# Quarter loads of expert weights, later reads of turned columns, and a rearranged attention prologue in a fused attention and expert kernel

## The chip, the core and the metric

The kernel runs on one core of a Trainium2 chip. The core has five engines with an instruction stream each: TensorE (PE: matmuls and transposes into PSUM), VectorE (DVE), ScalarE (ACT), GpSimd (POOL) and SyncE (SP, which only issues transfers here). They share the on-chip memory SBUF and meet through semaphores; every engine works through its own stream in order. Sixteen DMA engines move data. Transfers are issued by SyncE, ScalarE and GpSimd, each with a queue of its own. The metric is device time of one execution in microseconds, the median of several runs.

## What is computed

A polynomial sketch attention feeds a layer of experts chosen by a hash of the token number. Cut to what matters:

```python
# q, k, v: (4 batches, 4 heads, 1088 rows, 32); S1, S2: (8, 32)
phi(x) = outer(S1 x, S2 x)                  # 64 features of a row and head
kv, z  = sum_s phi(k)_s v_s^T, sum_s phi(k)_s
attn   = (phi(q) kv) / (phi(q) z + 1e-6)
x      = attn as rows: (4352, 128)          # the four heads side by side
e      = token_ids * 2654435761 % 8         # the expert of each row
out    = relu(x @ w1[e]) @ w2[e]            # w1: (8, 128, 1024), w2: (8, 1024, 128), float32
```

## The kernel before

**Attention.** One batch after the other. The 1024 main rows of a batch are eight tiles of 128, and 64 tail rows of each batch are kept in tiles of their own. For k and q, 128 x 128 blocks are turned on TensorE (`turned_all`, evicted by ScalarE), multiplied by the sketch matrix (`s_products`), and the outer product is made on VectorE in two products of 1024 columns (`features`, L512: `f` for q, `kp` for k). `values` (L532) copies v into a tile with a column of ones, on GpSimd. `kv_products` (L541) sums k's features times v, `q_turned` (L558, L565) turns q's features, `x_products` (L577) multiplies, `denominators` and `x_main`/`x_tail` (L603, L611) divide and store the rows to DRAM (`x_rows`). The loop `for b in range(B - 1)` (L757) works on the products of batch b and the features of batch b + 1; before it stand batch 0's first stages, k and q of batch 1 turned, and the tails' products and features (L732 to L746).

**Routing.** Beside the attention, VectorE and GpSimd work out where each row goes. `route_slots` gives a place, `route_rows` and `route_tiles` (L401) make 0/1 matrices for row and tile of that place, `tiles` (L411, L416, both on GpSimd) carries the token numbers in two parts, and `route_list` (L421) multiplies them on TensorE to a list `get` of tokens in the order of their experts, and `put`, where results go. Experts are taken in the order of how many rows are left beyond 256, from a table `order` that is worked out at run time; so a weight load first reads a register from `order` on the engine that issues it (`load_expert`).

**Experts.** There are 16 groups of rows: groups 0 to 7 have 256 rows each, one for each expert and only of batches 0 and 1; groups 8 to 15 hold the rest, 320 down to 271 rows. A group has eight steps c: `layer1(g, c)` (L837) makes 128 of the 1024 hidden columns and a ReLU evicts them, on ScalarE for even c and on VectorE for odd c (L623, L625); `layer2(g - 1, c)` (L845) adds the step's share of the group before. Four PSUM banks take turns in layer 1, two in layer 2.

Around these steps stand, at places written by hand as `at(group, step, function)`:

- `fetch_tile(k, j)`: gathers 128 rows by index on GpSimd (L617), its index copied on VectorE (`paced`, L677) to hold the gather back.
- Incoming rows are turned into columns: chunks 0 and 1 on TensorE (`bring`, L688), the others by `turn_in(k)`: VectorE splits them into halves of 16 bits (L696), SyncE issues one DMA transpose (L697), and `join_in(k)` puts them together again (L702, VectorE).
- Outgoing columns: ScalarE evicts in halves (L885), `turn_out` issues two DMA transposes on SyncE (L898), `join_out` joins them on VectorE (L906), `scatter_next` writes 128 rows by index from GpSimd (L848).
- `load_expert(r, ...)`: the two layers of the expert of rank r, 512 KB each. Ranks 0 to 2 go from SyncE; ranks 3 to 7 from ScalarE at step 2 of groups 1 to 5.
- `x_main`, `x_tail` of batches 2 and 3 on GpSimd, with their stores, in groups 1 and 2.

The order of each engine's instructions is that of the code (a manual schedule). VectorE waits in place when a joined tile has not landed, with the ReLUs behind it.

Of the kernel before, what the change touches and what calls it, by code (L numbers as in the profile page):

```python
# [9 lines left out]
F32 = mybir.dt.float32  # L10
BF16 = mybir.dt.bfloat16
I32 = mybir.dt.int32
# [18 lines left out]
def kernel(  # L31
# [13 lines left out]
    P = 128  # L45
# [102 lines left out]

    at_rank = {}
# [8 lines left out]
    q_tail = load_tail(q, "q_tail")  # L158
    k_t.append(load_main(k, 1, "k"))
    q_t.append(load_main(q, 1, "q"))  # L160
    v_tail = load_tail(v, "v_tail")
# [203 lines left out]
    def route_slots(digits):  # L365

        V_ = nc.vector
        late, slot, gap, over = (const.tile([P, C], F32, name=n) for n in ("late", "slot", "gap", "over"))
# [9 lines left out]
        V_.scalar_tensor_tensor(slot[:], slot[:], float((E - 1) * GE - (E - 2) * GAP), gap[:], op0=OP.add, op1=OP.add)  # L378
        V_.tensor_tensor(slot[:], slot[:], late[:], op=OP.mult)
# [28 lines left out]

    def route_tiles():
        hot(in_tile[:], number[:, 0:SE], st[:, 0])  # L410
        nc.gpsimd.tensor_tensor(tiles[:, :, 1].rearrange("p c (n x) -> p c n x", x=2),  # L411
                                in_tile[:].rearrange("p c (n x) -> p c n x", x=2),
                                twice[:].unsqueeze(2).to_broadcast([P, C, SE // 2, 2]), op=OP.mult)

    def route_tiles_p():
        nc.gpsimd.tensor_scalar(tiles[:, :, 0], in_tile[:], p1[:], None, op0=OP.mult)  # L416
# [113 lines left out]
    def values(b, copy=nc.gpsimd.tensor_copy):  # L530

        copy(vas[b % 2][:, :, :, 0:D], v_t[b][:].rearrange("p h t d -> p t h d"))  # L532
# [140 lines left out]
    def paced(idx):  # L673


        t = rows_in.tile([P, 1], I32, tag="idx", name="idx", bufs=4)
        nc.vector.tensor_copy(t[:], idx)  # L677
        return t[:]
# [43 lines left out]
    values(0)  # L722
# [6 lines left out]
    first_copied(aq, abq, range(GQ))  # L729
    kv = kv_products(0, kp, range(T))  # L730
    features(f, aq, abq, range(GQ))
    tail_ps = bank([P, 2, TT, P], "tail_ps")  # L732
    tail_turned(k_tail, tail_ps, 0)
    tail_turned(q_tail, tail_ps, 1)
    tailT = work.tile([P, 2, TT, P], F32, tag="fT", name="tailT", bufs=1)
    nc.scalar.copy(tailT[:], tail_ps[:])
# [3 lines left out]
    kT = turned_all(k_t[1], "kT")  # L740
    abt = tail_products(tailT)
    tail_features(abt)
    qT = turned_all(q_t[1], "qT")
    for u, va_tail in enumerate(va_tails):
        rows = tail_rows(u * TT)
        nc.gpsimd.tensor_copy(va_tail[rows, :, :, 0:D], v_tail[rows])  # L746
# [10 lines left out]
    for b in range(B - 1):  # L757
# [6 lines left out]
        if b == 0:  # L764
            k_t.append(load_main(k, 2, "k", A.memzero))
            q_t.append(load_main(q, 2, "q"))
            tail_f_turned()
            route_slots(digits)
        elif not last:
            qT = turned_all(q_t[b + 1], "qT")  # L770
# [3 lines left out]
        kv = kv_products(b, kp, range(T if b == 0 else 0, T + 1), kv if b == 0 else None)  # L774
        m = kv_diagonal(b, kv)
# [6 lines left out]
        values(b + 1)  # L782
        if b == 1:
            v_t.append(load_main(v, 3, "v", A.memzero))
            load_expert(0, (1,))
            route_rows(0)
            route_tiles()
            route_tiles_p()
            route_rows(1)
        features(f, aq, abq, range(GQ))  # L790
        x_products(b, fT, m)
# [5 lines left out]
        if b == 1:  # L797
            load_expert(0, (2,), A.memzero)
            load_expert(1, (1,))
        if b > 0:  # L800
            features(kp, ak, abk, range(GQ))
            denominators(b)
        else:
            denominators(b)
            features(kp, ak, abk, range(GQ))
        if not last:
            for g in range(GQ):
                x_main(b, g, nc.gpsimd)
            x_tail(b, nc.gpsimd)
        if last:  # L810
            for j in range(tiles_of(0)[1]):
                fetch_tile(0, j, True)

# [5 lines left out]
    load_expert(1, (2,), A.memzero)  # L819
    last_m = kv_diagonal(e, kv)  # L820
    for j in range(2):
        fetch_tile(1, j)

# [78 lines left out]
    def join_out():  # L902
        i, n, tts = turned_out.pop()
# [62 lines left out]
    for c in range(2):  # L966
        at(0, 3 + 2 * c, fetch_tile, 2, c)
    at(0, 4, load_expert, 2, (1, 2), lambda x: nc.vector.memset(x, 0.0))
    at(0, 6, bring, 1, o_bank)
    for g in range(1, E - 2):  # L970
        at(g, 2, load_expert, g + 2, (1, 2), None, nc.scalar, ENG.Activation)


    ahead = [(k, j) for k in range(3, 11) for j in range(tiles_of(k)[1])]
    for g, n in enumerate((0, 4, 4, 2, 2, 2, 2, 2)):
        for c in range(n):
            at(g, 1 + c, fetch_tile, *ahead.pop(0))
    assert not ahead

    for b, g in ((B - 2, 1), (e, 2)):  # L980
        for i in range(GQ):
            at(g, 5, x_main, b, i, nc.gpsimd, nc.gpsimd)
        at(g, 6, x_tail, b, nc.gpsimd, nc.gpsimd)
# [166 lines left out]
```

## Time and profile before

| | us |
|---|---|
| three runs | 191.65, 193.06, 193.37 |
| median | 193.06 |
| profiled execution, whole | 195.57 |
| its span, first to last instruction | 193.8 |
| attention until the first layer-1 product | 0 to 51.2 |
| experts | 51.2 to 193.8 |
| mean granted TensorE clock | 0.98 |

Durations below come from the profiled execution, 2.5 us longer than the median. Its page gives busy shares, the span in 40 slices (4.85 us each, a digit being tenths), and groups of instructions. In rows in order of time the columns are: start, length, engine, line and operation with its tiles and shapes, the number of instructions merged into the row, and in brackets how long the engine stood idle before it and what ended that. Lengths of merged rows run from the first start to the last end. What one execution spent in full-flow steps can be seen from 110 to 180 us, where TensorE is busy all the time:

```profile
65.40:98.70 33.30, 25.99 (x109) 21.46 (x108) 13.30 (x38) 7.78 (x22) 23.04 (x26) 0.95 0.73 187
110.00:180.00 70.00, 70.00 (x290) 54.44 (x289) 32.60 (x117) 19.27 (x52) 35.24 (x35) 1.00 0.30 69
```

Each row is a stretch (from, to, length), the busy time of TensorE, of its weight loads, of VectorE, ScalarE and GpSimd with their instruction counts, the granted clock, the share of the DMA engines, and GB/s.

### The profile page before, as it was taken

How to read it: one execution, taken by the hardware profiler on the slowest of the kernel's cores; microseconds unless marked ns; L12 is line 12 of the kernel's file. 1: busy time of each engine (PE TensorE's matmuls, PEld its weight loads, DVE VectorE, ACT ScalarE, POOL GpSimd, SP SyncE). 2: the span in 40 equal slices, each digit the busy share in tenths (PEclk: the TensorE clock that was granted, in tenths of full speed). 3: DMA queues.
4: the chain of work that ended last, by engine and by line, in shares of the span. 5: the costliest groups of instructions: out<-in, count | busy, mean ns of one | idle time of the engine just before them, and what ended most of it. 6: DMA issues, size and time to landing. Idle time of an engine off the chain costs nothing. (4 is left out here: it accounts for less than half of the span.)

```text
span 193.8 us, 4260 instructions
## 1 busy us (share of the span) xinstructions
PE 173.5 (90%) x1567; PEld 144.6 (75%) x1567; DVE 102.1 (53%) x291; ACT 63.2 (33%) x171; POOL 106.6 (55%) x145
## 2 busy tenths in 40 slices
PE   7788999799999569796959999999999999999990
PEld 3687999799887458575848888777777777778990
DVE  5786999989442283334233465263344654525330
ACT  3626674706352202222311332322313313231320
POOL 7251298974421877876526665644666444054752
PEclk9999999999999979999997999999999999999999
DMA  4994667961248927993889333414224052140111
GB/s 133 250 250 109 215 213 254 311 230 30 68 129 230 244 83 213 229 286 87 206 230 213 68 86 81 98 39 97 67 54 97 27 122 60 20 99 26 41 33 32
DMA packets 38678, 25.96 MB, mean 134 GB/s; under 512 B 21252, under 2 KB 35717, under 8 KB 38656
## 3 DMA queue, kind: packets, MB, share of 16 engines
q1 hardware_dynamic: 29952, 14.75, 29.1%
q0 software_dynamic: 2624, 5.64, 10.2%
q10 hardware_dynamic: 6080, 5.28, 10.0%
q8 instruction: 13, 0.21, 0.5%
q14 instruction: 9, 0.07, 0.1%
HBM read 17.41 MB, written 4.52 MB: 113 GB/s over the span
## 5 line engine op out<-in xcount | busy, mean ns | idle before, releaser
L845 PE MATMUL op<-hT,w 128*128 128x256 f32 (+8 forms) x256 | 78.2, 396 | 0.0
L625 DVE TENSOR_SCALAR hT<-hp 128x256 f32<-128x256 f32 (+9 forms) x68 | 29.0, 426 | 54.0 <-PE hp L837 44.3
L848 POOL DMA_INDIRECT out_dram<-os,put x35 | 35.3, 1008 | 40.2 <-DVE os L906 22.8
L845 PEld LDWEIGHTS op<-hT,w 128*128 128x128 f32 x256 | 48.6, 194 | 11.1
L623 ACT ACTIVATE hT<-hp 128x256 f32<-128x256 f32 (+9 forms) x68 | 26.6, 390 | 78.1 <-PE hp L837 76.6
L837 PE MATMUL hp<-xT,w 128*128 128x256 f32 x128 | 39.9, 401 | 9.8 <-DVE xT L702 6.0
L617 POOL DMA_INDIRECT xg<-x_rows,idx x33 | 33.7, 1020 | 23.1 <-DVE idx L677 11.2
L837 PE MATMUL hp<-xT_late,w 128*128 128x320 f32 (+8 forms) x144 | 41.7, 385 | 0.0
L837 PEld LDWEIGHTS hp<-xT,w 128*128 128x128 f32 x128 | 24.7, 199 | 15.7 <-DVE xT L702 6.8
L837 PEld LDWEIGHTS hp<-xT_late,w 128*128 128x128 f32 x144 | 25.3, 190 | 6.7
L906 DVE COPY os<-turned 128x256 uint16<-128x256 uint16 (+1 forms) x26 | 8.6, 358 | 9.1 <-DMA turned<-half 8.8
L696 DVE COPY xh<-xg 128x256 uint16<-128x256 uint16 (+1 forms) x28 | 9.0, 362 | 3.8 <-DMA xg<-x_rows,idx 3.8
L512 DVE TENSOR_TENSOR f<-first_of_ab,ab_ps 128x1024 f32<-128x1024 f32 x8 | 9.4, 1212 | 0.9 <-ACT first_of_ab L505 0.9
L512 DVE TENSOR_TENSOR kp<-first_of_ab,ab_ps 128x1024 f32<-128x1024 f32 x8 | 9.3, 1204 | 0.6 <-ACT first_of_ab L505 0.6
L541 PE MATMUL kv<-va,kp 128*64 128x33 f32 x256 | 8.4, 224 | 0.7 <-POOL va L532 0.7
L541 PEld LDWEIGHTS kv<-va,kp 128*64 128x64 f32 x256 | 7.9, 138 | 1.4 <-POOL va L532 0.8
L603 POOL TENSOR_TENSOR xs<-xe,den 128x512 f32<-128x512 f32 x8 | 8.3, 1055 | 0.7 <-DVE den L597 0.6
L702 DVE COPY xT<-xh_turned 128x256 uint16<-128x256 uint16 x12 | 4.9, 458 | 6.8 <-DMA xh_turned<-xh 6.6
L577 PE MATMUL x_ps<-m,fT 128*64 128x66 f32 x256 | 8.3, 222 | 0.0
L577 PEld LDWEIGHTS x_ps<-m,fT 128*64 128x64 f32 x256 | 7.9, 137 | 0.3 <-issue 0.3
L558 PE MATMUL fT_ps<-ident,f 128*128 128x128 f32 x64 | 7.9, 276 | 0.0
L885 ACT COPY half<-op 128x256 uint16<-128x256 uint16 x16 | 5.2, 375 | 7.3 <-PE op L845 7.3
(184 smaller groups left out, 171.3 us busy)
## 6 DMA issues: line engine op xcount, KB each, us to landing
w<-in_moe_w_dram ACTq DMA_DIRECT2D x10, 512.0 KB, 4.6
w<-in_moe_w_dram SPq DMA_DIRECT2D x6, 512.0 KB, 5.2
q<-in_q_dram SPq DMA_DIRECT2D x4, 512.0 KB
v<-in_v_dram SPq DMA_DIRECT2D x4, 512.0 KB, 6.9
k<-in_k_dram SPq DMA_DIRECT2D x3, 512.0 KB
x_rows<-xs SPq DMA_DIRECT2D x4, 256.0 KB, 4.0
x_rows<-xs POOLq DMA_DIRECT2D x4, 256.0 KB, 3.9
out_dram<-os,put POOLq DMA_INDIRECT x35, 2.8
```

The lines of the kernel that those rows point to most:

```text
L512: nc.vector.tensor_tensor(dst[:].rearrange("p t h i j -> p (t h) i j")[:, r], a[:, r].unsqueeze(3).to_broadcast(shape), rows_of_ab(ab)[:, ...
L541: nc.tensor.matmul(kv[h * R * R:(h + 1) * R * R, pr], f[:, 2 * pr + h].rearrange("p i j -> p (i j)"), v_[:, 2 * pr + h], start=(t == 0 and ...
L577: nc.tensor.matmul(p[r, t, 2 * pr:2 * pr + 2].rearrange("p h d -> p (h d)"), fT[:, lo + t, pr, r], m[:, pr].rearrange("p h d -> p (h d)"), ...
L603: eng.tensor_tensor(rows_of[b][:, r], xes[b % 2][:, r, 0:D], dens[b][:, r].unsqueeze(2).to_broadcast([P, Q * H, D]), op=OP.mult)
L617: nc.gpsimd.indirect_dma_start(out=dst, out_offset=None, in_=x_dram[0:rows], in_offset=bass.IndirectOffsetOnAxis(ap=idx, axis=0), bounds_c ...
L623: nc.scalar.activation(dst, src, AF.Relu if relu else AF.Copy)
L625: return nc.vector.tensor_scalar(dst, src, 0.0, None, op0=OP.max).ins
L696: nc.vector.tensor_copy(xh[:, x * w:(x + 1) * w], _half(xg3[k][:].rearrange("p a b -> p (a b)")[:, 0:w], x))
L837: nc.tensor.matmul(hp[:, 0:hi - lo], w1[:, g % E, c * P:(c + 1) * P], x_columns(first_of(g) + lo, first_of(g) + hi), start=True, stop=True)
L845: nc.tensor.matmul(ops[g][:, 0:hi - lo], w2[:, g % E, c], hTs[g][:, c, lo:hi], start=(c == 0), stop=(c == FC - 1))
L848: st_ = nc.gpsimd.indirect_dma_start(out=out[:], out_offset=bass.IndirectOffsetOnAxis(ap=idx, axis=0), in_=src, in_offset=None, bounds_che ...
L906: nc.vector.tensor_copy(_half(os[:].rearrange("p a b -> p (a b)"), x)[:, 0:n * DM], tts[x][:, 0:n].rearrange("p a b -> p (a b)"))
```

## The change

- **Weights.** `load_half` loads half a layer of an expert (256 KB, a quarter of the expert) from SyncE behind a VectorE memset of the destination's first column, which places it in time. In groups 1 to 6 the second layer of rank g + 1 comes at steps 0 and 3, the first layer of rank g + 2 at steps 4 and 7. Whole loads remain for ranks 0 and 1 and the first layer of rank 2, some at other places. Nothing is loaded from ScalarE any more.
- **Turned columns.** `turn_in(k)` moves to step 3 of group k - 2 (step 6 for k = 3 and k from 9), `join_in(k)` to step 4 of group k - 1. `join_out` moves to step 0 of the following group for g below 8, with the scatters after it; two turned tiles can be open, so the oldest is taken (`pop(0)`). Chunk 2 is turned on TensorE at (1, 5). Gathers move accordingly; their index tiles are eight instead of four.
- **Rows of batch 2** are divided on VectorE after the last `kv_diagonal`; those of batch 3 on GpSimd in group 0. Both are stored from SyncE.
- **Token numbers.** Of the two products that make `tiles`, one goes to VectorE, the other to ScalarE; the 0/1 matrix they need is made earlier, before the `kv_products` of batch 1.
- **Prologue.** Half of the first `values` goes to ScalarE, q's tail is loaded after the second q, and the tails are turned and made into features inside the first turn of the loop. `route_slots` is cut in two, `route_parts` coming first.

```diff
+    def load_half(r, layer, x):
+        load_expert(r, ())
+        e = at_rank[r]
+        if layer == 1:
+            r1 = slice(x * F // 2, (x + 1) * F // 2)
+            nc.vector.memset(w1[:, r, r1.start:r1.start + 1], 0.0)
+            nc.sync.dma_start(w1[:, r, r1], moe_w1[bass.ds(e, 1)].rearrange("o p f -> p (o f)")[:, r1])
+        else:
+            r2 = slice(x * FC // 2, (x + 1) * FC // 2)
+            nc.vector.memset(w2[:, r, r2.start, 0:1], 0.0)
+            nc.sync.dma_start(w2[:, r, r2], moe_w2[bass.ds(e, 1)].rearrange("o (c p) d -> p (o c) d", p=P)[:, r2])
...
     k_tail = load_tail(k, "k_tail")
-    q_tail = load_tail(q, "q_tail")
     k_t.append(load_main(k, 1, "k"))
     q_t.append(load_main(q, 1, "q"))
+    q_tail = load_tail(q, "q_tail")
...
+    def route_in_tile():
+        hot(in_tile[:], number[:, 0:SE], st[:, 0])
     def route_tiles():
-        hot(in_tile[:], number[:, 0:SE], st[:, 0])
-        nc.gpsimd.tensor_tensor(tiles[:, :, 1].rearrange("p c (n x) -> p c n x", x=2),
+        nc.vector.tensor_tensor(tiles[:, :, 1].rearrange("p c (n x) -> p c n x", x=2),
...
     def route_tiles_p():
-        nc.gpsimd.tensor_scalar(tiles[:, :, 0], in_tile[:], p1[:], None, op0=OP.mult)
+        nc.scalar.activation(tiles[:, :, 0], in_tile[:], AF.Copy, scale=p1[:])
...
-        t = rows_in.tile([P, 1], I32, tag="idx", name="idx", bufs=4)
+        t = rows_in.tile([P, 1], I32, tag="idx", name="idx", bufs=8)
...
-    values(0)
+    values(0, slice(0, T // 2))
...
     first_copied(aq, abq, range(GQ))
+    values(0, slice(T // 2, T), nc.scalar.copy)
...
         if b == 0:
...
-            tail_f_turned()
-            route_slots(digits)
+            tail_ps = bank([P, 2, TT, P], "tail_ps")
+            tail_turned(k_tail, tail_ps, 0)
+            tail_turned(q_tail, tail_ps, 1)
+            tailT = work.tile([P, 2, TT, P], F32, tag="tailT", name="tailT", bufs=1)
+            nc.scalar.copy(tailT[:], tail_ps[:])
+            qT = turned_all(q_t[1], "qT")
...
+            values(1)
+            route_parts(digits)
+            tail_features(tail_products(tailT))
...
+        if b == 1:
+            route_in_tile()
+            route_tiles_p()
...
         if b == 1:
             load_expert(0, (2,), A.memzero)
-            load_expert(1, (1,))
...
+        if b == 1:
+            load_expert(1, (1,))
         if last:
             for j in range(tiles_of(0)[1]):
                 fetch_tile(0, j, True)
+            load_expert(1, (2,), A.memzero)
...
-    load_expert(1, (2,), A.memzero)
     last_m = kv_diagonal(e, kv)
+    load_expert(2, (1,), A.memzero)
     for j in range(2):
         fetch_tile(1, j)
+    for g in range(GQ):
+        x_main(e - 1, g, V)
+    x_tail(e - 1, V)
...
-        i, n, tts = turned_out.pop()
+        i, n, tts = turned_out.pop(0)
...
     for c in range(2):
-        at(0, 3 + 2 * c, fetch_tile, 2, c)
-    at(0, 4, load_expert, 2, (1, 2), lambda x: nc.vector.memset(x, 0.0))
+        at(0, c, fetch_tile, 2, c)
+    for c in range(2):
+        at(0, 3 + c, fetch_tile, 3, c)
     at(0, 6, bring, 1, o_bank)
-    for g in range(1, E - 2):
-        at(g, 2, load_expert, g + 2, (1, 2), None, nc.scalar, ENG.Activation)
+    at(1, 5, bring, 2)
+    for g in range(1, E - 1):
+        for x in range(2):
+            at(g, 3 * x, load_half, g + 1, 2, x)
+            if g + 2 < E:
+                at(g, 4 + 3 * x, load_half, g + 2, 1, x)
...
-    ahead = [(k, j) for k in range(3, 11) for j in range(tiles_of(k)[1])]
-    for g, n in enumerate((0, 4, 4, 2, 2, 2, 2, 2)):
+    ahead = [(k, j) for k in range(4, 11) for j in range(tiles_of(k)[1])]
+    for g, n in enumerate((0, 2, 4, 4, 2, 2, 2)):
...
-    for b, g in ((B - 2, 1), (e, 2)):
-        for i in range(GQ):
-            at(g, 5, x_main, b, i, nc.gpsimd, nc.gpsimd)
-        at(g, 6, x_tail, b, nc.gpsimd, nc.gpsimd)
+    for i in range(GQ):
+        at(0, 5 + i, x_main, e, i, nc.gpsimd)
+    at(0, 7, x_tail, e, nc.gpsimd)
...
-    for k in range(2, G):
-        at(k - 1, 0, turn_in, k)
-        at(k - 1, 5, join_in, k)
+    for k in range(3, G):
+        at(k - 2, 3 if 3 < k <= E else 6, turn_in, k)
+        at(k - 1, 4, join_in, k)
     for g in range(2, G - 1):
         at(g, 1, turn_out, first_of(g - 1) // P)
-        at(g, 5, join_out)
-        for c in (6, 7):
-            at(g, c, scatter_next)
-        at(g + 1, 0, scatter_next)
+        c = FC if g < E else 5
+        for i, f in enumerate((join_out, scatter_next, scatter_next, scatter_next)):
+            at(g + (c + i) // FC, (c + i) % FC, f)
```

More of the change, by code (lines that the diff above doesn't have):

```diff
@@ L363, with route_parts @@
     place_t = const.tile([P, C], F32)
-    def route_slots(digits):
+    late, slot, gap, over = (const.tile([P, C], F32, name=n) for n in ("late", "slot", "gap", "over"))
+    def route_parts(digits):
         V_ = nc.vector
-        late, slot, gap, over = (const.tile([P, C], F32, name=n) for n in ("late", "slot", "gap", "over"))
         V_.tensor_scalar(place_t[:], digits[:], 2.0 ** -RB, WHOLE, op0=OP.mult, op1=OP.add)
@@ L378, in route_slots @@
         V_.scalar_tensor_tensor(slot[:], slot[:], float((E - 1) * GE - (E - 2) * GAP), gap[:], op0=OP.add, op1=OP.add)
+    def route_slots():
+        V_ = nc.vector
         V_.tensor_tensor(slot[:], slot[:], late[:], op=OP.mult)
@@ L528, in feature_tile, with values @@
         return hots.tile([P, T, H, R, R], F32, tag=tag, name=tag, bufs=1)
-    def values(b, copy=nc.gpsimd.tensor_copy):
-        copy(vas[b % 2][:, :, :, 0:D], v_t[b][:].rearrange("p h t d -> p t h d"))
+    def values(b, ts=slice(0, T), copy=nc.gpsimd.tensor_copy):
+        copy(vas[b % 2][:, ts, :, 0:D], v_t[b][:, :, ts].rearrange("p h t d -> p t h d"))
     def kv_products(b, kp, ts, kv=None):
@@ L729 @@
     first_copied(aq, abq, range(GQ))
+    values(0, slice(T // 2, T), nc.scalar.copy)
     kv = kv_products(0, kp, range(T))
     features(f, aq, abq, range(GQ))
[L732 to L736, printed above, removed]
+    kT = turned_all(k_t[1], "kT")
     route_bases(cnt)
@@ L739 @@
     route_order_end()
[L740 to L746, printed above, removed]
     fT_tail = const.tile([P, TT, H // 2, P], F32)
@@ L766 @@
             q_t.append(load_main(q, 2, "q"))
-            tail_f_turned()
-            route_slots(digits)
+            tail_ps = bank([P, 2, TT, P], "tail_ps")
[4 more added lines that the diff above has]
+            qT = turned_all(q_t[1], "qT")
+            for u, va_tail in enumerate(va_tails):
+                rows = tail_rows(u * TT)
+                nc.gpsimd.tensor_copy(va_tail[rows, :, :, 0:D], v_tail[rows])
+            values(1)
+            route_parts(digits)
+            tail_features(tail_products(tailT))
         elif not last:
@@ L773 @@
             route_end(idx)
-        kv = kv_products(b, kp, range(T if b == 0 else 0, T + 1), kv if b == 0 else None)
-        m = kv_diagonal(b, kv)
+        if b == 1:
+            route_in_tile()
+            route_tiles_p()
+        if b > 0:
+            kv = kv_products(b, kp, range(T + 1))
+            m = kv_diagonal(b, kv)
         abq, aq, f = ab_bank(), first_of_ab(), feature_tile("f")
@@ L781 @@
         first_copied(ak, abk, range(GQ))
-        values(b + 1)
+        if b == 0:
+            kv_products(0, None, range(T, T + 1), kv)
+            m = kv_diagonal(0, kv)
+            tail_f_turned()
+        else:
+            values(b + 1)
         if b == 1:
@@ L787 @@
             route_tiles()
-            route_tiles_p()
             route_rows(1)
         features(f, aq, abq, range(GQ))
+        if b == 0:
+            route_slots()
         x_products(b, fT, m)
@@ L798 @@
             load_expert(0, (2,), A.memzero)
-            load_expert(1, (1,))
-        if b > 0:
+        if last:
             features(kp, ak, abk, range(GQ))
```

## The prediction

> **What bounds the kernel now.** I read the page's busy shares and slices first, then TensorE's order of time for its holes, then the rows of VectorE, ScalarE and SyncE at the same moments. The chain of waits is of no use here: it ends after four pieces in the last 6 us.
>
> ```profile
> PE 173.5 (90%) x1567; PEld 144.6 (75%) x1567; DVE 102.1 (53%) x291; ACT 63.2 (33%) x171; POOL 106.6 (55%) x145
> ...
> PE   7788999799999569796959999999999999999990
> DVE  5786999989442283334233465263344654525330
> ...
> PEclk9999999999999979999997999999999999999999
> DMA  4994667961248927993889333414224052140111
> ```
> TensorE is the bound: 173.5 of 193.8 us. Its holes lie at the start and in slices 13 to 21 (61 to 105 us), the first experts, where the DMA engines are at 7 to 9 tenths; from 105 us on there is none. In two of these slices the granted clock falls to 7. TensorE in order of time:
>
> ```profile
> 69.44 0.70 PE L837 MATMUL hp<-xT,w 128*128 128x256 f32 x2 [3.85 <-DVE xT L702]
> ...
> 72.43 1.06 PE L837 MATMUL hp<-xT,w 128*128 128x256 f32 x2
> ...
> 82.23 0.70 PE L837 MATMUL hp<-xT,w 128*128 128x256 f32 x2 [1.35 <-DVE hT L625]
> ...
> 88.94 0.70 PE L837 MATMUL hp<-xT,w 128*128 128x256 f32 x2 [2.12 <-DVE xT L702]
> ...
> 100.64 1.11 PE L837 MATMUL hp<-xT,w 128*128 128x256 f32 x2 [1.94 <-DVE hT L625]
> ```
> With a fifth hole of 0.42 at 62.73 they are 3.85 + 1.35 + 2.12 + 1.94 + 0.42 = **9.68 us**. A pair of layer-1 matmuls starts every 0.43 us in full flow; after 69.44 and after 100.64 six pairs take 4.38 us in place of 2.59, at half clock: 2 x 1.79 = **3.6 us**. Each hole waits for VectorE, so I ask what VectorE waited for:
>
> ```profile
> 61.85 0.49 DVE L696 COPY xh<-xg 128x256 uint16<-128x256 uint16 x2 [3.76 <-DMA xg<-x_rows,idx]
> ...
> 67.29 2.09 DVE L702 COPY xT<-xh_turned 128x256 uint16<-128x256 uint16 x2 [3.40 <-DMA xh_turned<-xh]
> ...
> 80.54 1.32 DVE L906 COPY os<-turned 128x256 uint16<-128x256 uint16 x1 [3.15 <-DMA turned<-half]
> ...
> 88.37 0.52 DVE L702 COPY xT<-xh_turned 128x256 uint16<-128x256 uint16 x2 [3.25 <-DMA xh_turned<-xh]
> ...
> 99.54 0.73 DVE L906 COPY os<-turned 128x256 uint16<-128x256 uint16 x2 [4.71 <-DMA turned<-half]
> ```
> Always a late gather or DMA transpose, in front of which VectorE stands in order and leaves the ReLUs behind it. Why late, from ScalarE's and SyncE's rows:
>
> ```profile
> 91.88 0.34 ACTq L143 DMA_DIRECT2D w<-in_moe_w_dram  x1
> 92.38 0.46 ACTq L147 DMA_DIRECT2D w<-in_moe_w_dram  x1
> ...
> 92.15 2.62 SPq L898 DMA_TRANSPOSE turned<-half  x2
> ```
> A whole expert (1 MB) is thrown at the 16 engines just as the transposes start; those were read at 99.54, though the median transpose of this kind lands 2.5 us after its issue (longest 6.5).
>
> **The change, part by part.** A "step" is one layer-1 and one layer-2 product of 256 columns, 0.43 + 0.43 = 0.86 us; a group of eight, 6.9 us.
>
> *Third chunk turned on TensorE.* Chunk 2 takes two TensorE transposes (0.38 us, the row of chunk 1 at 56.81) and one ScalarE copy (0.38), and its two gathers come five and four steps earlier in the first group. Its DMA transpose goes. The 3.85 us hole goes with its chain; cost 0.4 us.
>
> *Later reads.* Incoming columns are read nine steps (7.8 us) behind their transpose (six for chunk 3 and from 9 on), where it was five; outgoing ones seven steps (6.0 us) instead of four. In the holes of 1.35 and 1.94 VectorE stood 3.5 us (77.39, end of the first copy, to the hole at 80.88) and about 4 us (94.8 to 98.7) before TensorE ran dry, so some 3 us more are free. An outgoing column must thus land over 9 us after its issue to stop TensorE; before, the longest took 6.5. All four remaining holes go.
>
> *Quarter loads.* Ten loads from ScalarE's queue and one load of expert 2's second layer become 22 of 256 KB on SyncE's, each behind a VectorE memset (0.06 us, row L968). 22 x 0.06 = 1.3 us of VectorE over six groups of 41 us in which it is 30 to 50% busy: nothing, and if that cover went, 0.2 us a group. ScalarE loses ten issues of 0.35 to 0.46 in 13 us of slack: nothing. SyncE gains per group four issues (spacing 0.54 at 56.25 and 56.79, so 2.2 us) and a register load (under 0.3, ScalarE's gap at 60.6). With one transpose in and two out at 1.2 us and 0.1 between (3.9) SyncE is taken for 6.4 of 6.9 us. It holds, narrowly. The pieces are wanted at least eleven steps (9.5 us) after their issue. The first pieces are queued behind the last x rows, which wait for GpSimd (its 2.5 us of division end near 59 by my shift of its rows, against 83.3 before); they have ten us to spare.
>
> *Amount of DMA.* From 65.4 to 98.7 the engines were busy 0.73 of 33.3 us, 24.3 us for four groups: 6.1 us each; TensorE at full pace gives 6.9. So 88% full.
> [...] The row: slice 17, with one whole expert and transposes, moved 286 GB/s, and halves of 512 KB issued together landed in a median 4.6 us. [...]
>
> *Rows of expert batch 2 divided on VectorE* instead of GpSimd, and their store on SyncE. VectorE idled 2.13 us before 52.46; two of these (1.06 on GpSimd; bounds 0.6, half of the 1.2 of a 1024-wide product, and 1.06) and a tail are 1.5 to 2.5 us; I take 1.6. Covered; without cover the first ReLU is 0.5 late, inside the 3 us above. The stores of both last batches leave GpSimd's queue (3.6 us of issuing between 69 and 84) for SyncE's, six issues of 0.3 to 0.6 there before its load of pieces begins. Both divisions now come before group 1; between 67 and 81 us they stood beside VectorE copies that took 1.89 and 1.32 instead of 0.36.
>
> *Attention.* Rows: the wait at 11.29 (0.71, on GpSimd's copy of v) is cut to about 0.2 by giving half to ScalarE, which has 3 us idle there. The index product waited for GpSimd:
>
> ```profile
> 38.99 1.26 PE L421 MATMUL idx_ps<-tiles,row 128*128 128x72 bf16 x34 [1.30 <-POOL tiles L416]
> ...
> 30.00:40.00 10.00, 8.70 (x198) 8.45 (x195) 9.96 (x11) 6.00 (x16) 8.66 (x5) 1.00 0.87 291
> ```
> (the second: from, to, length, TensorE, its loads, VectorE, ScalarE, GpSimd, clock, DMA). GpSimd loses 3.23 + 3.39. VectorE, the real bound of this stretch at 9.96, gains one bf16 product of 1224 elements: at least 0.7 (the 1.28 of 2176 elements scaled), at most 1.97, its neighbour slowed by GpSimd; I take 1.0. ScalarE gets the other, some 1.2 us where it idles 1.62 before 30.09. VectorE saves 0.9 on L596 (1.07 in place of 0.18 beside GpSimd) and 0.8 because the tail's product and slots now fill its 1.19 us hole at 18.43. Tails moved behind the second q put q's 0.94 us wait at 16.37 under other work, but TensorE then waits for the tail's product on VectorE near 20 us: even. Walking both engines through, f of the third batch starts near 43.0 instead of 43.94: **1.0 us gained**, bounds -1 (the product at 1.97 and ScalarE's copy late) and +1.3.
>
> **Sum.** 9.7 + 3.6 - 0.4 + 1.0 = 13.9 us. At 88% DMA and 93% SyncE one hole of the mildest kind seen will, I estimate, be left: -1.3. So 12.6: span 193.8 to 181.2, profiled time 195.57 to 183.0. The median shown, 193.06, is 2.5 below that profiled run; the same step gives 180.5, and as undisturbed runs may stall a little less to begin with, **181**.
>
> [...] The row: half clock after holes of 3.85 and 1.94, none after 2.12 or 1.35. [...] The trace decides for 3.6; it also says that a left hole of 2 us may cost 3.8.
>
> **The rivals.**
> (a) *The DMA engines stay the limit*: at 88% a few reads are still late. For it: slices 16 to 19 at 8, 9, 9, 3; against: weights have 9 us of lead. Three holes of 1.4 and one spell of half clock, 6 us: 187.
> (b) *VectorE or the tail chain binds attention*: for it 9.96 of 10; the lower bound -1: 183.
> (c) *Transposes caught in SyncE's own queue: slower.* Before, weights had another queue than transposes; now a pair of outgoing transposes follows two pieces (512 KB) in the same one, on an issuer 93% taken. If columns come later than 9 us after they are ready, each group 2 to 7 has a hole; at 2 us plus 1.8 of half clock that is 6 x 3.8 = 23 us on 178.5: 201. It decides from about 10.5 us a column; for it the 6.5 seen; against, that 6.5 came with a whole megabyte ahead and here it is half of one.
> (d) *The pieces are not spread*, memsets running early or SyncE bunching them: then contention stays but reads are later; about as (a).
>
> **How the numbers follow.** Holes gone, with 1.3 left or nothing (and b): 0.62, 178.5 to 184. (a) and (d): 0.25, 184 to 192. No difference within 1% (about what a measurement can tell), with the end of (a): 0.05. (c): 0.08. The range 178 to 188 leaves out 0.2. Faster 0.87, within 1% 0.05, slower 0.08.
>
> **What would show it.** TensorE from 56 to 105 us without holes over 1 us, clock 9 in slices 13 to 22, group 2 starting near 63.6 instead of 69.44; no wait of VectorE over 3 us for a turned tile; index product without its 1.30. Wrong would be: waits of TensorE for weights, of VectorE for turned tiles at every group, or a SyncE whose transposes are issued over 2 us after their columns are ready.

## The result, and the profile after

| | before | after |
|---|---|---|
| runs | 191.65 to 193.76 | 182.6, 183.56, 183.64, 185.93 |
| median | 193.22 | 183.6 |
| span of the profiled run | 193.8 | 183.7 |
| spans of the other runs | | 180.4, 181.4, 181.5 |
| first layer-1 product, in the profiled run | 51.2 | 54.7 |
| from there to the end | 142.5 | 129.0 |

The ratio is 0.948, interval 0.940 to 0.956: faster, by 9.6 us. The profiled run is the longest of the four, 2.3 us above their median, and has something in it that the others need not have; the changed kernel was therefore run again, beside the kernel before (runs `a1_again`, `c2_again`, `d2_after` below). Some runs of a kernel are longer than its others, so the medians and ranges of the experiments are those of the runs within 1.5% of the fastest of their kernel. `a1_again` gave 181.9 against 193.8, a ratio of 0.939, 0.927 to 0.952.

The page of the changed kernel, the same rows that were shown of before (busy shares, then the span in slices of 4.6 us):

```profile
PE 172.5 (94%) x1569; PEld 146.1 (80%) x1569; DVE 97.7 (53%) x312; ACT 65.6 (36%) x175; POOL 93.6 (51%) x134
...
PE   6999896799899799999999999999999999999990
...
DVE  4689979865793323445445443533355573333330
...
PEclk9999999699999999999999999999999999999999
DMA  4994629079247359999999932152231413120110
```

TensorE's busy time hardly moved (173.5 to 172.5): it was the idle time that went. The holes of slices 13 to 21 are gone but for a 7 in slice 13 (0.82 us ahead of chunk 1, which waits for a gather), and so are the two slices of low clock there. In their place stand a 6 and a 7 at slices 6 and 7 (counted from 0), with a 6 in the clock at slice 7: a hole in the attention that was not there before. The DMA engines now work through in slices 15 to 22, where before they had pauses.

The experts in full flow, as a window (from, to, length; busy time of TensorE, its weight loads, VectorE, ScalarE, GpSimd; clock, DMA share, GB/s), after:

```profile
62.00:97.00 35.00, 34.87 (x163) 30.68 (x163) 15.44 (x79) 10.25 (x29) 23.37 (x24) 1.00 0.96 212
```

and before, over the same 35 us:

```profile
62.00:97.00 35.00, 27.26 (x115) 22.51 (x114) 14.98 (x47) 7.99 (x23) 25.04 (x28) 0.95 0.73 192
```

TensorE is busy for 34.87 of 35 us instead of 27.26. The same transfers are packed into less time: a share of 0.96 in place of 0.73. At this share TensorE stood idle for 0.13 us in all. Whether anybody stood and waited for a landing can be read from VectorE's reads of turned columns, in order of time (start, length, operation, and in brackets idle time before it with its cause):

```profile
80.49 0.50 DVE L722 COPY xT<-xh_turned 128x256 uint16<-128x256 uint16 x2
...
83.38 0.52 DVE L941 COPY os<-turned 128x256 uint16<-128x256 uint16 x1
83.81 0.29 DVE L941 COPY os<-turned 128x256 uint16<-128x256 uint16 x1
...
90.67 0.37 DVE L941 COPY os<-turned 128x256 uint16<-128x256 uint16 x1 [0.30 <-DMA turned<-half]
91.26 0.31 DVE L941 COPY os<-turned 128x256 uint16<-128x256 uint16 x1 [0.22 <-DMA turned<-half]
```

Before, such rows carried waits of 3.15 to 4.71 us; from 60 to 112 us the waits for turned tiles are now 0.5 us in all, in two rows. SyncE, a full group of it:

```profile
76.88 0.96 SPq L156 DMA_DIRECT2D w<-in_moe_w_dram  x2
78.08 0.38 SPq L160 DMA_DIRECT2D w<-in_moe_w_dram  x1
78.57 2.50 SPq L933 DMA_TRANSPOSE turned<-half  x2
81.32 0.40 SPq L160 DMA_DIRECT2D w<-in_moe_w_dram  x1
81.81 1.20 SPq L717 DMA_TRANSPOSE xh_turned<-xh  x1
83.86 0.95 SPq L156 DMA_DIRECT2D w<-in_moe_w_dram  x2
```

From 76.88 to 83.86 is one group, 83.86 - 76.88 = 6.98 us. The issues in it are 0.96 + 0.38 + 2.50 + 0.40 + 1.20 = 5.4 us, 78% of it, where I had reckoned 6.4 and 93%.

Then the new hole. TensorE around slices 6 and 7, after:

```profile
29.91 0.78 PE L510 MATMUL ab_ps<-s_k,qT 128*64 128x64 f32 x18
33.33 1.02 PE L510 MATMUL ab_ps<-s_k,qT 128*64 128x64 f32 x14 [2.64 <-issue]
34.03 2.02 PE L510 MATMUL ab_ps<-s_k,kT 128*64 128x64 f32 x32
```

It stands in the midst of one product of 32 equal matmuls: 18 are done, then nothing for 2.64 us, then the other 14. They have the same operands and the same bank, so no tile and no buffer is what the nineteenth waited for, and the profile agrees: "issue" is a wait that it sees no cause of. The next product takes 2.02 instead of the 1.10 of `a1_again` below, at half clock (granted 0.50 from 34.03 to 36.05 us). Together they make most of the 3.4 us by which the experts start later than before.

### The profile page after: what moved, and what is told of

Same layout as the page of the kernel before. It is cut to its first block, busy times and chain, and to the rows that moved or that the text cites. A ratio compares the mean times of both kernels' runs of the same rounds, so it can differ in the third digit from the quotient of the medians.

```text
span 183.7 us, 4336 instructions
## 1 busy us (share of the span) xinstructions
PE 172.5 (94%) x1569; PEld 146.1 (80%) x1569; DVE 97.7 (53%) x312; ACT 65.6 (36%) x175; POOL 93.6 (51%) x134
## 5 line engine op out<-in xcount | busy, mean ns | idle before, releaser
L880 PE MATMUL op<-hT,w 128*128 128x256 f32 (+8 forms) x256 | 76.3, 389 | 0.0
L880 PEld LDWEIGHTS op<-hT,w 128*128 128x128 f32 x256 | 47.5, 190 | 10.5
L872 PE MATMUL hp<-xT,w 128*128 128x256 f32 x128 | 37.6, 381 | 0.1
L872 PEld LDWEIGHTS hp<-xT,w 128*128 128x128 f32 x128 | 24.0, 191 | 3.6 <-issue 0.5
L623 POOL TENSOR_TENSOR xs<-xe,den 128x512 f32<-128x512 f32 x6 | 6.2, 1049 | 8.8 <-ACT kT L486 8.8
L597 PE MATMUL x_ps<-m,fT 128*64 128x66 f32 x256 | 8.8, 228 | 0.0
L597 PEld LDWEIGHTS x_ps<-m,fT 128*64 128x64 f32 x256 | 8.4, 144 | 0.5 <-ACT w L142 0.3
L941 DVE COPY os<-turned 128x256 uint16<-128x256 uint16 (+1 forms) x26 | 7.5, 327 | 1.2 <-DMA out_dram<-os,put 0.6
L510 PE MATMUL ab_ps<-s_k,qT 128*64 128x64 f32 x128 | 5.2, 235 | 2.8 <-issue 2.6
L578 PEld LDWEIGHTS fT_ps<-ident,f 128*128 128x128 f32 x64 | 7.1, 141 | 0.1
```

What stands on the lines that cost most here:

```text
L578: nc.tensor.transpose(p[:, t, pr], f[:, 2 * i + t, 2 * pr:2 * pr + 2].rearrange("p h i j -> p (h i j)"), ident[:])
L597: nc.tensor.matmul(p[r, t, 2 * pr:2 * pr + 2].rearrange("p h d -> p (h d)"), fT[:, lo + t, pr, r], m[:, pr].rearrange("p h d -> p (h d)"), ...
L623: eng.tensor_tensor(rows_of[b][:, r], xes[b % 2][:, r, 0:D], dens[b][:, r].unsqueeze(2).to_broadcast([P, Q * H, D]), op=OP.mult)
L872: nc.tensor.matmul(hp[:, 0:hi - lo], w1[:, g % E, c * P:(c + 1) * P], x_columns(first_of(g) + lo, first_of(g) + hi), start=True, stop=True)
L880: nc.tensor.matmul(ops[g][:, 0:hi - lo], w2[:, g % E, c], hTs[g][:, c, lo:hi], start=(c == 0), stop=(c == FC - 1))
L941: nc.vector.tensor_copy(_half(os[:].rearrange("p a b -> p (a b)"), x)[:, 0:n * DM], tts[x][:, 0:n].rearrange("p a b -> p (a b)"))
```

## The experiments

There are twelve runs of nine kernels, in four lots; in each, the kernel before ran on the same chip. Its medians in the four lots are 193.8, 191.1 (from only two runs; five others took 194.6 to 198.8), 198.7 and 200.5, so times are compared within a lot first. The theory to test was mine: later reads and quarter loads together take the holes away. Its rivals were that one of the two does it alone, and, for the attention, that the new hole at 30 us belongs to the change and not to the run.

### The changed kernel again, and the loads of k and q moved

`a1_again` is the changed kernel without an edit.

> The changed kernel once more. Theory F (TensorE runs out of instructions while the DMA engines are full, near 30 us, where the loads of the fourth k and q and the stores of x rows are in flight): its profile has a hole of 1 to 3 us in the middle of the sketch products of q near 30 us again, put down to no releaser, and half clock after it; time 183 to 184. Rival (an accident of one execution): no such hole, time 180 or less.

`a2_early` moves the last loads of k and q, which stand in the queue just before the hole, some ten us ahead:

```diff
+            k_t.append(load_main(k, 3, "k"))
+            q_t.append(load_main(q, 3, "q"))
...
-            k_t.append(load_main(k, 3, "k"))
-            q_t.append(load_main(q, 3, "q"))
```

> Fourth k and q loaded right after the second q has been turned (near 18 us) instead of behind the third v (near 25 us). Theory F: the DMA engines are no longer full at 30 us, the hole of 2.6 us and the half clock behind it go, first layer-1 product near 50.5 instead of 54.7, time 179 to 180.5. Rival (the hole is a wait for ScalarE's product of tile numbers or for VectorE's long product of 2.46 us, both at the same moment): hole stays, time 183 to 184.

Measured: 181.9 (180.8 to 182.8), between the two times expected, and 182.7 (182.3 to 183.2), so nothing was gained by moving the loads. In `a1_again` the place of the hole and its surroundings read:

```profile
30.42 1.13 PE L510 MATMUL ab_ps<-s_k,qT 128*64 128x64 f32 x32
31.38 1.10 PE L510 MATMUL ab_ps<-s_k,kT 128*64 128x64 f32 x32
...
50.33 1.13 PE L872 MATMUL hp<-xT,w 128*128 128x256 f32 x4
...
58.15 0.33 PE L708 MATMUL xp<-ident,xg 128*128 128x128 f32 x1 [1.97 <-DMA xg<-x_rows,idx]
```

No hole at 30 us, and layer 1 starts at 50.33, 0.9 us ahead of before and 4.3 ahead of the first profile of the very same code. So the hole belongs to the run and not to the change. `a2_early` had two short ones (0.17 and 1.09 us), and one of them again after 18 of the 32.

That position is the clue. Over all profiles, the holes put to "issue" inside a run of equal matmuls in the attention stood here:

| run | after 18 of 32, third product of q (L510) | after 2 of 32, fourth product of q (L510) | at the third product of the tails (L606) |
|---|---|---|---|
| first profile | 2.64 | | 0.47, after 2 of 4 |
| `a1_again`, `a3_whole`, `a4_close`, `b2_w1_later`, `b5_tiles_pool` | none | none | none |
| `a2_early` | 0.17 | | 1.09, after 2 of 4 |
| `b1_neither` | 2.64 | | 0.81, after 2 of 4 |
| `c2_again` | | 0.79 | 0.40, 5 matmuls sooner |
| `d1_w1_later` | | 1.31 | 0.39, 4 sooner |
| `d2_after` | | 0.19 | 0.37, 7 sooner |
| `c1_best` | | none | 0.42, 3 sooner |

Counting the matmuls in TensorE's rows, the second place lies 254 behind the first, and the third 128 behind the second. Each brings a weight load, so these are 508 and 256 instructions (the short holes of the later lots lie a few matmuls off). The page lists a transfer queue called "instruction" with 13 packets and 0.21 MB, 16 KB a packet. Whose instructions it carries, the page does not say. If they were TensorE's alone, its 1569 matmuls and 1569 weight loads over 13 packets would make 241 a packet, an estimate by which the places lie about two packets and one apart. The traces hold each packet of this queue (the DMA view over a narrow window shows it), so its landing can be set beside the moment at which TensorE goes on:

| profile, place | packet starts, lands | TensorE goes on | after the landing |
|---|---|---|---|
| first profile, first place | 30.76, 31.87 | 33.33 | 1.5 |
| `b1_neither`, first | 31.38, 32.48 | 33.88 | 1.4 |
| `a2_early`, first | 28.91, 30.20 | 31.53 | 1.3 |
| `c2_again`, second | 39.07, 40.32 | 41.78 | 1.5 |
| `d1_w1_later`, second | 40.79, 41.96 | 43.41 | 1.5 |
| `a2_early`, third | 45.02, 45.98 | 47.23 | 1.3 |
| `a1_again`, first: no stop | 25.00, 25.93 | 30.97 | 5.0 |

The same holds for the three other stops exactly at these places (1.2 to 1.5 us), and in none of the twelve profiles in which these instructions stand in this order does TensorE pass one of the three places sooner than 1.2 us after its packet has landed. Of the four short stops a few matmuls sooner two end 1.2 to 1.3 us after a landing, and two (`c1_best`, `d2_after`) do not fit. So I take it that in these stops TensorE waited for its own instructions; what speaks for it are these times and the queue's name. The expectation of `c2_again` had called a stop at another place a sign against this; the one that came lies 508 instructions behind the first place, and ended 1.5 us after a packet of the same queue had landed.

Why the packet comes late in some runs is less sure. From 27 to 32 us the DMA engines were full in the first profile and in `a1_again` alike (shares of 0.99 to 1.16 and 1.03 to 1.10 in each microsecond). In `a1_again` the packet had passed ahead of that stretch; in the first profile it came near its end; in `a2_early`, without the loads of k and q there, the engines were full only to 28 us, and it came at 28.91. So a packet that comes behind the loads is the likely cause. Why it comes ahead of them in one run and behind them in another is not shown.

### Which half of the change takes the expert holes away

Three kernels complete a two by two with `a1_again` (late reads, quarter loads). `a3_whole` keeps the late reads and loads each expert whole from ScalarE at step 2, as before:

```diff
-    for g in range(1, E - 1):
-        for x in range(2):
-            at(g, 3 * x, load_half, g + 1, 2, x)
-            if g + 2 < E:
-                at(g, 4 + 3 * x, load_half, g + 2, 1, x)
+    at(0, 4, load_expert, 2, (2,), lambda x: nc.vector.memset(x, 0.0))
+    for g in range(1, E - 2):
+        at(g, 2, load_expert, g + 2, (1, 2), None, nc.scalar, ENG.Activation)
```

> Quarter loads undone: ranks 3 to 7 loaded whole from ScalarE at step 2 of groups 1 to 5, as before; late reads kept. If late reads alone take the holes away (nine and seven steps plus 3 us of slack against 7.4 us at worst): no hole over 1 us from 62 to 105 us, time within 1 us of the changed kernel (183 to 184). If the spreading of the loads is needed too: transposes land 6 to 8 us after their issue, VectorE waits 1 to 3 us for turned tiles, one or two holes, 185 to 189.

`a4_close` keeps the quarter loads and puts the reads back to five steps (incoming) and four (outgoing):

```diff
-        at(k - 2, 3 if 3 < k <= E else 6, turn_in, k)
-        at(k - 1, 4, join_in, k)
+        at(k - 1, 0, turn_in, k)
+        at(k - 1, 5, join_in, k)
...
-        c = FC if g < E else 5
+        c = 5
```

> Late reads undone: turned tiles read five and four steps behind their transposes again, quarter loads kept. If quarters alone suffice, transposes land within 4 us and VectorE's slack of 3 us covers the rest: 183 to 185. If the distance decides: holes of 1 to 2.5 us in several of groups 2 to 6 with half clock after some, 187 to 193.

`b1_neither` has both edits, and so the rest of the change alone.

> Both undone: whole loads from ScalarE and reads five and four steps behind; chunk 2 on TensorE, rows of batch 2 on VectorE and the prologue as changed. Late reads alone were enough (no hole in full flow with whole loads, 181.7), quarter loads with close reads left four holes, 3.8 us (187.5). If quarters halve the waits where reads are close: without them holes of 6 to 9 us and some half clock, 188 to 193. If quarters do nothing in either place: 187 to 188.

| median us | quarter loads | whole loads |
|---|---|---|
| late reads | 181.9 (`a1_again`, 180.8 to 182.8) | 181.4 (`a3_whole`, 181.2 to 181.9) |
| close reads | 187.4 (`a4_close`, 186.0 to 187.6) | 188.2 (`b1_neither`, 187.9 to 188.7) |

The last is of the second lot, the others of the first. Within the first lot, putting the reads back costs 5.5 us with quarter loads, and putting the loads back costs nothing where the reads are late. With whole loads putting the reads back costs 6.8 us, across two lots; within the second, `b1_neither` is 5.8 us above `b3_late_only` (182.4, below), which has late reads and whole loads but not the rest of the change. The window of full flow in `a3_whole`:

```profile
62.00:97.00 35.00, 35.00 (x165) 30.79 (x164) 16.32 (x65) 10.81 (x31) 21.41 (x21) 1.00 0.98 226
```

No idle time at all, at a DMA share of 0.98 with whole megabytes. In `a4_close` TensorE has four holes, together 3.84 us:

```profile
82.34 0.67 PE L872 MATMUL hp<-xT,w 128*128 128x256 f32 x2 [2.14 <-issue]
90.05 0.67 PE L872 MATMUL hp<-xT,w 128*128 128x256 f32 x2 [0.56 <-ACT half L920]
98.04 0.67 PE L872 MATMUL hp<-xT,w 128*128 128x256 f32 x2 [0.85 <-ACT half L920]
105.48 0.67 PE L872 MATMUL hp<-xT,w 128*128 128x256 f32 x2 [0.29 <-issue]
```

and each follows a wait of VectorE in front of an incoming turned tile, the old picture:

```profile
81.73 0.52 DVE L722 COPY xT<-xh_turned 128x256 uint16<-128x256 uint16 x2 [3.22 <-DMA xh_turned<-xh]
...
89.43 0.52 DVE L722 COPY xT<-xh_turned 128x256 uint16<-128x256 uint16 x2 [1.64 <-DMA xh_turned<-xh]
...
97.42 0.52 DVE L722 COPY xT<-xh_turned 128x256 uint16<-128x256 uint16 x2 [1.93 <-DMA xh_turned<-xh]
...
104.86 0.51 DVE L722 COPY xT<-xh_turned 128x256 uint16<-128x256 uint16 x2 [1.38 <-DMA xh_turned<-xh]
```

`b1_neither` has four holes, 0.65 + 1.91 + 0.98 + 0.91 = 4.45 us. The holes differ by 0.6 us, the medians by 0.8, from two lots; so little if anything is left for the quarter loads even where the reads are close. Neither has a hole in the full groups before 79 us: the one of 3.85 us in front of group 2 went with chunk 2 turned on TensorE and its earlier gathers, as forecast, and not with the later reads.

Distance counts because a landing is only waited for where it is read too soon. In `a4_close` incoming columns were waited for at five steps (1.4 to 3.2 us in the lines above) and outgoing ones at four (0.3 to 1.0 us); in `a1_again`, at nine and seven, the longest such wait to 112 us is 0.63. In `a2_early` it is 2.5, without a hole of TensorE behind it: the 3 us that I had counted as slack beyond the steps were there. Whether transposes also landed sooner or more evenly can't be told: of the outgoing ones in the experts' stretch the trace of before gives the landing of 4 in 10 (2.6 to 6.5 us after issue), that of `a1_again` of 2 in 14 (4.4 and 5.2).

### The late reads alone

`b3_late_only` is the kernel before, with only what the later reads need: the moved gathers with eight index tiles, chunk 2 turned on TensorE, and the oldest turned tile taken first. Loads, the rows of batch 2 and 3, token numbers and prologue stay as before.

> The kernel before with later reads alone (turned tiles nine, six or seven steps behind, gathers moved to fit, chunk 2 turned on TensorE); whole loads, x rows, token numbers and prologue as before. If late reads carry nearly all of the gain: holes of 61 to 105 us gone, 183 to 185, about 10 us below before. If GpSimd, with the divisions of two batches and their stores in groups 1 and 2 beside the earlier gathers, takes their place: chunks 3 to 5 late, holes of 2 to 4 us, 186 to 190.

Measured: 182.4 (180.6 to 183.3), 8.7 us below the 191.1 beside it. No hole is left in the experts' flow. What is left stands ahead of it:

```profile
37.80 1.27 PE L421 MATMUL idx_ps<-tiles,row 128*128 128x72 bf16 x34 [1.26 <-POOL tiles L416]
...
49.84 0.33 PE L688 MATMUL xp<-ident,xg 128*128 128x128 f32 x1 [1.00 <-DMA xg<-x_rows,get]
...
51.73 2.08 PE L837 MATMUL hp<-xT,w 128*128 128x256 f32 x4
```

The index product waits for GpSimd as before (1.26 us), and then the second gather of chunk 0 is late; behind it the first four matmuls of layer 1 take 2.08 instead of 1.13, at half clock. The whole change with one load moved, in the same lot, took 180.8 (`b2_w1_later`, below). So one part carries nearly all of the gain, and the rest is worth a microsecond or two. That part is itself three things, incoming reads, outgoing reads and chunk 2 on TensorE; no run takes the incoming and the outgoing reads apart.

### The token numbers back on GpSimd

`b5_tiles_pool` undoes one part of the rest: both products that make `tiles` return to GpSimd, and the matrix they need goes behind the first row matrix.

```diff
-        nc.vector.tensor_tensor(tiles[:, :, 1].rearrange("p c (n x) -> p c n x", x=2),
+        nc.gpsimd.tensor_tensor(tiles[:, :, 1].rearrange("p c (n x) -> p c n x", x=2),
...
-        nc.scalar.activation(tiles[:, :, 0], in_tile[:], AF.Copy, scale=p1[:])
+        nc.gpsimd.tensor_scalar(tiles[:, :, 0], in_tile[:], p1[:], None, op0=OP.mult)
```

> The changed kernel with the two products of token numbers back on GpSimd, and the 0/1 matrix back behind the first row matrix. Theory: the index product of TensorE waits 1 to 1.5 us for GpSimd again and VectorE loses 0.9 on a division beside it, 1 to 2 us more than the changed kernel, 183 to 184. Rival (the attention is bound elsewhere, by VectorE's features, and the wait is absorbed): within 0.5 us of the changed kernel.

Measured: 186.9 (186.3 to 187.7), 5 us more than the changed kernel in the first lot and 6 more than `b2_w1_later` in its own: far beyond what I expected. VectorE, then GpSimd, then TensorE:

```profile
36.63 3.33 DVE L616 TENSOR_SCALAR den<-xe 128x36 f32<-128x36 f32 x1
...
40.29 2.29 DVE L532 TENSOR_TENSOR kp<-first_of_ab,ab_ps 128x1024 f32<-128x1024 f32 x2
```

```profile
33.32 3.23 POOL L431 TENSOR_TENSOR tiles<-in_tile,twice 128x1224 bf16<-128x1224 bf16 x1 [0.73 <-DVE in_tile L419]
36.54 3.39 POOL L436 TENSOR_SCALAR tiles<-in_tile,p 128x1224 bf16<-128x1224 bf16 x1
40.52 2.05 POOL L623 TENSOR_TENSOR xs<-xe,den 128x512 f32<-128x512 f32 x2 [0.60 <-DVE den L617]
...
47.85 1.28 POOL L637 DMA_INDIRECT xg<-x_rows,get  x1 [3.94 <-DVE f L532]
```

```profile
39.98 1.27 PE L441 MATMUL idx_ps<-tiles,row 128*128 128x72 bf16 x34 [1.22 <-POOL tiles L436]
...
51.86 0.33 PE L708 MATMUL xp<-ident,xg 128*128 128x128 f32 x1 [0.91 <-DMA xg<-x_rows,get]
53.31 0.33 PE L708 MATMUL xp<-ident,xg 128*128 128x128 f32 x1 [1.12 <-DMA xg<-x_rows,get]
```

An operation on 36 columns, 0.20 us in the changed kernel, takes 3.33 us: it starts 0.09 us behind GpSimd's product and ends 0.03 us behind it (36.63 + 3.33 = 39.96 against 36.54 + 3.39 = 39.93). What held VectorE's operation until GpSimd's had ended, the rows do not show. In the kernel before, `kp` stood ahead of `den`, and the same division took 1.07.

But this delay is not what costs the 5 us. Layer 1 starts at 55.25, against 50.33 in `a1_again`, because the first gather is issued at 47.85 instead of 43.66, and the gather waits for the rows of batch 1 in DRAM. (The profile names VectorE's `f` for that wait, but GpSimd's queue was released at 46.8 us, when the last of these rows landed.) GpSimd divides the rows only behind its own two products: at 40.52 instead of 38.02, of which the delayed division is 0.6 and GpSimd's own work the rest. The store of the tail rows then landed 3.8 us after its issue (1.8 in the kernel before), and the first gather 3.9 (2.8 in `a1_again`). TensorE's index product came 1.9 us later, at 39.98 instead of 38.06, straight behind GpSimd's second product, and `kp` held it up for another 0.26. So roughly half of the 5 us is the two products in GpSimd's line; the other half is slower transfers, whose cause is not shown. The kernel before and `b3_late_only` have the products on GpSimd too and start layer 1 at 51.23 and 51.73.

### The hole ahead of chunk 1

In `a1_again` one hole is left near the experts' start, the 1.97 us shown above: the second gather of chunk 1 lands late, beside a load of 512 KB (the first layer of the second expert) issued just ahead of it. `b2_w1_later` issues that load at step 4 of group 0:

```diff
-    load_expert(2, (1,), A.memzero)
...
+    at(0, 4, load_expert, 2, (1,), lambda x: nc.vector.memset(x, 0.0))
```

> The changed kernel with the first layer of rank 2 (512 KB) loaded at step 4 of group 0 instead of ahead of chunk 1's gathers. Theory: that load, issued within 1 us of the gathers, makes the second gather land 5 to 6 us late and leaves the hole of 0.8 to 2.0 us before chunk 1 is turned; hole gone, 1 to 2 us less than the changed kernel, 180 to 181. Rival (GpSimd gets its indices too late): hole of 0.8 to 2 us stays, 182 to 183.

Measured: 180.8 (180.3 to 181.1), and the hole is gone. That looked like a version that beats the changed kernel, so it was run with the whole loads (`c1_best`), and then by itself (`d1_w1_later`), each beside the changed kernel without an edit (`c2_again`, `d2_after`).

> The changed kernel with two edits that ran alone before: whole loads of an expert's weights, issued on ScalarE (181.67 alone), and the first layer of the second expert loaded one step later, behind chunk 1's gathers (180.95 alone). If the hole ahead of chunk 1's transposes is that load's doing whatever issues the others, it is gone here too, and the two together give 180 to 181, 1 to 1.5 us below the changed kernel beside it, with expert holes of zero. If whole loads bring their own collisions once the later load moves, a hole of 1 us or more comes back and the time is 181.5 to 183.

> The changed kernel once more, as the mark for the run beside it: 181 to 184; near 181.9 where TensorE has no hole in the midst of the product of 32 instructions at about 30 us, near 183.6 where it has one of 2 to 3 us with the half clock behind it. The same instruction positions (behind 18 of the 32 and behind 2 of the 4 of the softmax sum) are where a hole may stand; a hole at another place would speak against instruction loading as its cause.

> The changed kernel with the first layer of the second expert loaded one step later, now timed beside the changed kernel itself. If that load makes the hole of 1.5 to 2 us ahead of chunk 1's transposes, this is 0.5 to 1.5 us faster than the run beside it: 181 where that is 182, whatever the transfers of the lot are like otherwise. If the hole came with the lot and not with the load, both are within 0.3 us.

> The changed kernel as the mark. In a lot like the first, 181.9 with no hole from 62 to 97 us; if transfers are as late as in the third lot, near 189 with holes of 1 us and more at 86, 97 and 110 us. Ahead of chunk 1's transposes a hole of 1.5 to 2 us.

| lot | kernel before | changed kernel | other |
|---|---|---|---|
| third | 198.7 | 189.6 (`c2_again`, 189.4 to 191.4) | 187.9 (`c1_best`, 187.3 to 189.7) |
| fourth | 200.5 | 189.0 (`d2_after`, 188.5 to 191.2) | 190.3 (`d1_w1_later`, 189.8 to 192.3) |

Neither is shown to be better. The ratios to the kernel before overlap in both lots: 0.943 (0.932 to 0.954) beside 0.956 (0.946 to 0.966), and 0.953 (0.946 to 0.959) beside 0.947 (0.940 to 0.954). The profiles of the changed kernel in these lots, and that of `a2_early` in the first, have no hole ahead of chunk 1 although the load stands where it stood, so the load does not make the hole by itself; that theory falls in the form in which I had it.

All kernels were slower in these two lots than in the first, the one before by 5 and 7 us and the changed one by 8 and 7; their ratio was 0.956 and 0.947. In the changed kernel there are holes again. Full flow in `d2_after`, and its two larger holes there (a third is 0.18):

```profile
62.00:97.00 35.00, 32.59 (x149) 27.46 (x148) 13.89 (x68) 9.09 (x26) 22.30 (x23) 1.00 0.81 206
```

```profile
85.71 0.70 PE L872 MATMUL hp<-xT,w 128*128 128x256 f32 x2 [0.46 <-DVE idx L697]
...
96.83 0.83 PE L872 MATMUL hp<-xT,w 128*128 128x256 f32 x2 [1.77 <-issue]
97.44 1.06 PE L880 MATMUL op<-hT,w 128*128 128x256 f32 x2
```

The engines moved about as many bytes a second as in the first profile (206 GB/s against 212) at a lower share. These are not the old holes: in front of them VectorE and ScalarE stand idle ahead of a ReLU, not ahead of a turned tile.

```profile
93.48 0.38 ACT L643 ACTIVATE hT<-hp 128x256 f32<-128x256 f32 x1 [3.95 <-PE hp L872]
...
96.34 0.42 DVE L645 TENSOR_SCALAR hT<-hp 128x256 f32<-128x256 f32 x1 [5.83 <-PE op L880]
```

`c1_best`, `c2_again` and `d1_w1_later` show the same: in each, both engines stood for 3.7 to 6.7 us ahead of a ReLU. The products that these ReLUs evict stand in TensorE's rows some microseconds earlier; what held the ReLUs back, the traces do not show, and in that of `d2_after` no landing of a transfer can be read in the experts' stretch. It stays open, and so does what made these two lots slower.

## Why the prediction was right, and where not

Forecast 181 with a range of 178 to 188; measured 183.6, and 181.9 in the first lot of repeats. By its steps:

- **The expert holes, 9.7 + 3.6 - 0.4, less 1.3 for one left.** The sum is 11.6. From the first layer-1 product to the end it was 142.5 before, 129.0 in the first profile and 130.2 in `a1_again`: 13.5 and 12.4 gained (before rounding). The mechanism was right, and both spells of half clock went with the holes. The 1.3 I kept back was about the hole that `a1_again` has, 1.97, but that stands ahead of chunk 1 and not, as I had it, in the full groups; so group 2 starts at 66.25 there, not near 63.6.
- **Why they go.** I gave the later reads the four remaining holes and the quarter loads the evening out of traffic. The first is shown by the two by two (5.5 us within a lot) and by `b3_late_only` (8.7 us, with chunk 2 on TensorE). The second was not needed: 181.4 with whole loads, 181.9 with quarters.
- **Quarter loads, nothing lost.** Right: those quarters of the first profile whose landing can be read took a median 3.4 us with DMA 96% full, where the halves of 512 KB issued from ScalarE took 4.6 before, and quarters and whole loads gave the same time.
- **Half clock, 3.6.** It again followed short holes: 1.00 us in `b3_late_only`, and 0.91 with 1.12 in `b5_tiles_pool` (in both the first four matmuls of layer 1 took 2.08 us instead of 1.13); but none followed 1.97 in `a1_again` (granted clock 1.00 from 53.25 to 180 us). Before, it followed a hole of 1.94 and not one of 2.12, so in these profiles the length of a single hole does not decide it. The gain was real: from 62 to 106 us the granted clock was 0.92 before and is 1.00 after, and 0.08 x 44 is 3.5 us.
- **Amount of DMA, 88% full.** Measured 0.96 from 62 to 97 us, and no harm came of it. Two readings of the page were off: in slices 13 to 21 the DMA row stands at 2 in slice 14 and at 3 in slice 18, not at 7 to 9 throughout, and slices 16 to 19 read 9, 9, 3, 8, not 8, 9, 9, 3.
- **SyncE 6.4 of 6.9.** Measured 5.4 of 6.98. I took a spacing of 0.54 for each load; two issued together took 0.96, one 0.38 to 0.40.
- **Attention, 1.0.** 0.9 in `a1_again` (51.23 to 50.33), and minus 3.4 in the first profile; `a3_whole` and `a4_close`, with the same attention, start layer 1 at 48.94 and 50.55, so a single profile tells this term only to a microsecond or more. The terms: row products of batch 2 on VectorE 1.28 + 0.29 = 1.57 (predicted 1.6), VectorE's product of token numbers 0.78 (1.0), ScalarE's 1.32 (1.2). What failed here is a term that the sum did not have, a stop of TensorE between two instructions of one product, with half clock after it: layer 1 started at 54.7 in the first profile, which has it, and at 50.33 in `a1_again`, which has not. With it the profiled run's span is 183.7 where the sum said 181.2; the other three have 180.4 to 181.5. That the whole came so close has some luck in it: the experts gave one to two microseconds more than their 11.6, which hid part of this.
- **What I priced too low** was the move of the token numbers off GpSimd: put back, they cost 5 us, about half of it because the rows of batch 1 stand behind them on GpSimd and the first gather behind those rows. I had counted TensorE's wait and VectorE's division, not this chain.
- **The rivals.** SyncE's queue did not hold the transposes back (a full group has 1.5 us free), the attention did not lose the 1 us of (b) except by TensorE's stop, and the pieces were spread as written. The DMA limit, my (a) at 187, did not show in the first two lots. The third and fourth have times of 188 to 190 and holes of 0.4 to 1.8 us, but behind late ReLUs at a DMA share of 0.8, which is not what (a) described.

## What to carry to other kernels

Where an engine that works in order reads a transfer's result in front of other work, first lengthen the distance between issue and read: here it took four more index tiles and was worth 5 to 9 us, where splitting the transfers was worth nothing. Before work is moved to an engine, look at what stands behind it in that engine's line: two products of 3.3 us on GpSimd put off the rows behind them, and with them the first gather. And before explaining a hole by the change, run the same code again; for a hole inside a row of equal instructions, look at the packets of the queue called "instruction": here TensorE went on 1.2 to 1.5 us after one had landed.

## What the runs showed of the hardware that I had not expected

- TensorE stopped for 0.17 to 2.64 us between two matmuls that depend on nothing new, in some runs of a kernel and not in others. At three places, 508 and 256 instructions apart, it went on 1.2 to 1.5 us after a packet of 16 KB of the queue called "instruction" had landed.
- A VectorE `tensor_scalar` of 36 columns, 0.20 us in the changed kernel, took 3.33 us beside a GpSimd instruction of 3.39 us and ended 0.03 us behind it (`b5_tiles_pool`).
- 22 loads of 256 KB and 11 of 512 KB gave the same time, 181.9 and 181.4 us, at a DMA share of 0.98 (`a1_again`, `a3_whole`).
